# Banded attention and a top-1 mixture of experts on one core: the list of slots spread over the experts' steps, and GpSimd's instructions pinned in the order given

## The chip, the cores and the metric

The kernel runs on one core of one Trainium2 chip. The metric is device time in microseconds (us) of one execution; the number that counts is the median of several runs. An execution has a span (from the first to the last instruction on the core) and a little time around it.

## The reference

Attention over 8 batches, 8 heads, 576 positions and 64 channels. The first four heads see a plain window of 32 positions, the other four a window of 128 positions with a stride of 4. The result, 4608 tokens of 512 channels, goes through a gate that picks one of 8 experts for each token, and through that expert's two layers. Cut to what matters:

```python
scores = where(mask, q @ k.T / sqrt(64), -1e9)
attn = softmax(scores); x = (attn @ v) as 4608 x 512
logits = x @ w_gate + modality_bias[modality_id]
e_idx = argmax(logits); gate_w = softmax(logits)[e_idx]
out[e_idx == e] = gate_w * (relu(x[e_idx == e] @ w1[e]) @ w2[e])
```

## The kernel before, in words

**Attention** is cut into 72 units of 128 rows (nine a batch). A unit's steps lie in different turns of the main loop: `scores` (PE matmuls into `pss`, the mask and the row maximum `nmx` on DVE, and the subtraction `sm` on GpSimd, line 274 by way of the helper `pool`), then `exp` on ACT, `probsT`, `attend`, `normalize`, `store`, and `logits`. Each unit's rows `x_sb` are also written to the scratch tensors `x_dram` by DMAs that GpSimd issues.

**Routing.** When a batch's logits are there, `gating` finds the expert of each token, its place in the expert's list, and scatters token numbers and gate weights into `table` (line 493, six indirect DMAs a batch, issued by GpSimd). Slots of 256 tokens of one expert are the unit of the experts' work. After batch 4 a first list of three slots (0, 1 and 2) is made, so that the experts' work can begin beside the attention's last units. After the last batch `slot_info` makes the list of all other slots and `rest_info` that of the last half slot (`info` and `info_h`, lines 513 to 598: together 37 very small DVE operations on one partition, in pieces that are separated by `yield`). Slots 3 and later cannot be fetched before that list exists.

**A slot's rows** come in a chain: SyncE (SP) reads the slot's place from the list and loads its token numbers (`idt`, line 622); GpSimd gathers the rows with four indirect DMAs into `xr`; SP writes `xr` to the scratch `x_slot` (line 641) and loads it back rearranged as `xg` (four DMAs, line 647); `prepare_x` transposes `xg` on DVE to `xt` (line 786), and ACT and DVE split it into `xh` and `xl` (lines 792 and 793), for each half of 128 tokens in turn. `xr`, `xg` and `xt` have one buffer each.

**The experts' work** is the generator `slots`. A slot has eight groups (f = 0 to 7). A group has 12 matmuls 128x256 of the first layer (line 854), the activation `hh` on ACT and its remainder `hl` on DVE, then the six matmuls 128x512 of the second layer (line 834) of the group two before, then the splits of a piece of `w2` and of the `w1` piece for two groups later (`w2h`, `w1h` on ACT, `w2l`, `w1l` on DVE, lines 802 and 803). A group yields four times, so four steps of the generator make one group. After the second group of a slot, the last slot's two outputs `ys` are scattered to `out` by GpSimd. The helper `ahead`, called twice a group, fetches lists, rows and weights; from the fourth group (f = 3) on it advances `prepare_x` of the next slot, one piece a group. `hold` keeps a slot from being given out before its rows are prepared: it calls `ahead` until they are.

**What sets the order.** PE, DVE, ACT and SP run in the order in which the program gives the instructions (a manual schedule). GpSimd's instructions are placed by a scheduler; the class `InOrder` (line 269) marks them to be kept in program order, and the scatters of `table` are tied to the instruction given last. At the end of the main loop `while not state['routed']` (line 1014) alternates one step of the experts' work with two pieces of the routing of the last batch.

Of the kernel before, what the change touches and what calls it, by code (L numbers as in the profile page):

```python
# [64 lines left out]
def kernel(  # L65
# [53 lines left out]
    def load_qk(b, kd, queue=nc.sync):  # L119
        kn = load_one(b, kd, k)  # L120
        return load_one(b, kd, q, queue), kn
# [17 lines left out]
    state = {('qk', 0, 0): load_qk(0, 0, nc.scalar)}  # L139
# [129 lines left out]
    class InOrder:  # L269


        def __getattr__(self, name):
            def issue(*args, **kw):
                ins = tc.keep_in_program_order(getattr(nc.gpsimd, name)(*args, **kw))  # L274
                state['pool'] = ins.ins
                return ins
            return issue

    pool = InOrder()
# [392 lines left out]
    order = []  # L672
# [250 lines left out]
    def step(share=MOE_RATE / 6):  # L923

        nonlocal credit
        if moe:
            credit += share if state['t'] < NU else 1
            while credit >= 1:
                credit -= 1
                next(moe, None)  # L930

    def advance(some=range(-1, B)):
        for b, task in tasks:
            if b in some:
                next(task, None)
# [76 lines left out]


    while not state['routed']:
        step(1)
        advance()
        advance()
    run(moe)
    man.close()
# [34 lines left out]
```

## Time and profile before

| what | us |
|---|---|
| median of three runs | 710.94 |
| the three runs | 710.84, 721.43, 710.94 |
| the profiled execution | 717.6 |
| its span | 715.9 |
| PE busy in the span | 652.0 (91%) |
| DVE, ACT, GpSimd busy | 496.2, 455.5, 290.7 |

The attention fills about the first 250 us, the experts' work the rest. The two overlap from about 258 us to 287 us; slot 1 of the experts begins at 285 us, slot 2 at 318 us, slot 3 at 341 us. The trace gives, for each instruction, its start, its length, and what ended the idle time of its engine before it.

### The profile page before, as it was taken

The page shows a single profiled execution, that of the slowest core. Times are in us where ns is not written, and L with a number is a line of the kernel's source. Part 1 is how long each engine was busy: PE and PEld are TensorE (multiplying, and loading weights), DVE is VectorE, ACT ScalarE, POOL GpSimd, SP SyncE. Part 2 cuts the span into 40 slices and gives each one's busy share as a digit, 9 for nine tenths or more (in the row PEclk, how much of TensorE's full clock was granted, in tenths as well). Part 3 has the DMA queues.
Part 4 walks back from the last instruction along what each step waited for, and adds up shares of the span by engine and source line. Part 5 has one row for each costly group of instructions (what it writes and reads, how often), then busy time and mean ns, then how long its engine had stood idle before and what let it go on. Part 6 is the DMA issues. An engine that isn't in the chain of part 4 may idle for free. (4 is left out here: it accounts for less than half of the span.)

```text
span 715.9 us, 17885 instructions
## 1 busy us (share of the span) xinstructions
PE 652.0 (91%) x6286; PEld 572.8 (80%) x6286; DVE 496.2 (69%) x1212; ACT 455.5 (64%) x964; POOL 290.7 (41%) x396
## 2 busy tenths in 40 slices
PE   6898899996988789879999999999999999999991
PEld 3687777775876578779999989999999899999880
DVE  1678788785787788687666766677666776667660
ACT  4698799895767665436656555656665565665650
POOL 7344766764658654433333232333213231310110
PEclk7699999999789899989999999999999999999996
DMA  9897698697856964213333863233232336821730
GB/s 163 144 224 176 156 193 177 136 189 131 166 123 159 242 161 79 89 51 98 118 108 100 247 170 115 75 104 119 73 106 75 104 118 169 220 82 46 197 90 12
DMA packets 163233, 94.95 MB, mean 133 GB/s; under 512 B 124144, under 2 KB 143090, under 8 KB 163140
## 3 DMA queue, kind: packets, MB, share of 16 engines
q1 hardware_dynamic: 146612, 63.89, 40.1%
q0 software_dynamic: 11120, 28.64, 13.2%
q10 hardware_dynamic: 5408, 1.24, 1.1%
q8 instruction: 51, 0.84, 0.5%
q14 instruction: 42, 0.34, 0.2%
HBM read 127.52 MB, written 29.39 MB: 219 GB/s over the span
## 5 line engine op out<-in xcount | busy, mean ns | idle before, releaser
L854 PE MATMUL pt<-xh,w1l 128*128 128x256 f32 (+1 forms) x608 | 172.6, 284 | 7.5 <-DVE w1l L803 7.5
L854 PE MATMUL pt<-xl,w1h 128*128 128x256 f32 (+1 forms) x608 | 172.1, 283 | 0.0
L854 PE MATMUL pt<-xh,w1h 128*128 128x256 f32 (+1 forms) x608 | 172.0, 283 | 0.0
L860 ACT ACTIVATE hh<-pt 128x256 fp32r<-128x256 f32 (+1 forms) x152 | 57.6, 379 | 160.3 <-PE pt L854 160.2
L803 DVE TENSOR_TENSOR w2l<-w2q,w2h 128x512 fp32r<-128x512 f32 x152 | 104.8, 689 | 43.1 <-ACT w2h L802 34.7
L274 POOL DMA_INDIRECT xr<-x_dram,idt x74 | 82.8, 1118 | 121.4 <-DMA x_slot<-xr 70.5
L854 PEld LDWEIGHTS pt<-xh,w1l 128*128 128x128 f32 x608 | 116.5, 192 | 8.4 <-DVE w1l L803 8.4
L854 PEld LDWEIGHTS pt<-xh,w1h 128*128 128x128 f32 x608 | 116.4, 191 | 7.2 <-ACT w1h L802 0.6
L854 PEld LDWEIGHTS pt<-xl,w1h 128*128 128x128 f32 x608 | 116.4, 191 | 5.7
L834 PE MATMUL py<-w2h,hh 128*128 128x512 f32 x296 | 118.3, 400 | 0.0
L834 PE MATMUL py<-w2h,hl 128*128 128x512 f32 x296 | 117.2, 396 | 0.0
L834 PE MATMUL py<-w2l,hh 128*128 128x512 f32 x296 | 116.2, 393 | 0.0
L861 DVE SCALAR_TENSOR_TENSOR hl<-pt,hh 128x256 fp32r<-128x256 f32 (+1 forms) x152 | 63.2, 416 | 74.9 <-ACT hh L860 74.9
L274 POOL DMA_INDIRECT out_dram<-ys,idt x37 | 39.8, 1076 | 178.7 <-ACT ys L837 115.8
L803 DVE TENSOR_TENSOR w1l<-w1q,w1h 128x512 fp32r<-128x512 f32 x152 | 103.8, 683 | 3.0 <-ACT w1h L802 3.0
L802 ACT CAST w1h<-w1q 128x512 fp32r<-128x512 f32 x152 | 94.5, 622 | 3.6 <-DMA w1q<-in_moe_w_dram 3.6
L802 ACT CAST w2h<-w2q 128x512 fp32r<-128x512 f32 x152 | 93.1, 612 | 0.0
L274 POOL TENSOR_TENSOR sm<-sm,nmx 128x384 f32<-128x384 f32 x72 | 59.9, 832 | 64.4 <-DVE den L368 49.3
L361 PE MATMUL po<-vw,pT 96*64 96x65 f32 x1152 | 55.9, 239 | 20.3 <-ACT pT L355 16.5
L361 PEld LDWEIGHTS po<-vw,pT 96*64 96x64 f32 x1152 | 44.6, 147 | 32.7 <-ACT pT L355 20.9
L834 PEld LDWEIGHTS py<-w2l,hh 128*128 128x128 f32 x296 | 55.9, 189 | 13.3
L834 PEld LDWEIGHTS py<-w2h,hh 128*128 128x128 f32 x296 | 56.4, 190 | 6.7
(160 smaller groups left out, 1119.9 us busy)
## 6 DMA issues: line engine op xcount, KB each, us to landing
w2q<-in_moe_w_dram SPq DMA_DIRECT2D x76, 512.0 KB
w1q<-in_moe_w_dram SPq DMA_DIRECT2D x152, 256.0 KB
st<-in_k_dram SPq DMA_DIRECT2D x64, 144.0 KB
x_slot<-xr SPq DMA_DIRECT2D x18, 512.0 KB
xg<-x_slot SPq DMA_DIRECT2D x72, 128.0 KB
x_dram<-x_sb POOLq DMA_DIRECT2D x32, 256.0 KB, 3.6
st<-in_q_dram SPq DMA_DIRECT2D x56, 144.0 KB
vw<-in_v_dram SPq DMA_DIRECT2D x8, 576.0 KB
```

The source lines that it names most:

```text
L274: ins = tc.keep_in_program_order(getattr(nc.gpsimd, name)(*args, **kw))
L361: nc.tensor.matmul(out=pov[u * TQ:(u + 1) * TQ, h, :], lhsT=self.pT[:, h, u * TQ:(u + 1) * TQ], rhs=self.vts[kd][:, h, i, :], start=True, ...
L802: nc.scalar.copy(out=hi, in_=raw)
L803: nc.vector.tensor_tensor(out=lo, in0=raw, in1=hi.bitcast(F32), op=ALU.subtract)
L834: nc.tensor.matmul(out=py[u], lhsT=ht[:, us], rhs=wt, start=(f + n == 0), stop=(f + n == FC + 1))
L854: nc.tensor.matmul(out=ph, lhsT=wt[:, c, :], rhs=xt[:, c, 0:cols], start=(c + i == 0), stop=(c + i == KC + 1))
L860: nc.scalar.activation(out=hh, in_=ph, func=AF.Relu)
L861: nc.vector.scalar_tensor_tensor(out=hl, in0=ph, scalar=0.0, in1=hh.bitcast(F32), op0=ALU.max, op1=ALU.subtract)
```

## The change: one piece of routing per three steps, and GpSimd tied

The loop that ends the routing now takes three steps of the experts' work and then one piece of routing, where it took one step and two pieces. Besides, each instruction that goes through the helper `pool` is tied, in the schedule alone and without a semaphore, to the one given before it.

```diff
@@ class InOrder
                 ins = tc.keep_in_program_order(getattr(nc.gpsimd, name)(*args, **kw))
+                if 'pool' in state:
+                    tc.add_manual_dep(ins.ins, state['pool'].name, mybir.DependencyInfo(mybir.DependencyClass.NoSync, mybir.DependencyReason.SCHED_ONLY),
+                                      reason="GpSimd's order")
                 state['pool'] = ins.ins
                 return ins
@@ after the main loop
     while not state['routed']:
-        step(1)
-        advance()
+        for _ in range(3):
+            step(1)
         advance()
     run(moe)
```

Lines after the first hunk are three higher in the changed kernel. The first place that changes is GpSimd's queue near the end of the attention. `sm` is the subtraction that a unit's exponential waits for, `table` a scatter, `xr_5256` the gathers of slot 1's rows. Before:

```order
L493 DMA table_87<-pay_266,dst_4544 41472x3
L274 DMA xr_5256<-x_dram0_84,idt_4215 128x256
L274 DMA xr_5256<-x_dram1_85,idt_4215 128x256
L274 DMA xr_5256<-x_dram0_84,idt_4215 128x256
L274 TENSOR_TENSOR sm_4647<-sm_4647,nmx_4648 128x384
L493 DMA table_87<-pay_266,dst_4544 41472x3
L274 DMA xr_5256<-x_dram1_85,idt_4215 128x256
L274 TENSOR_TENSOR sm_4731<-sm_4731,nmx_4732 128x384
```

Slot 1's four gathers stood here before and between two units' subtractions. In the changed kernel `sm_4647` follows the scatter at once, and the gathers come after the very last subtraction of the attention, `sm_5174`:

```order
L496 DMA table_87<-pay_266,dst_5145 41472x3
L274 TENSOR_TENSOR sm_5174<-sm_5174,nmx_5175 128x384
L274 DMA x_dram0_84<-x_sb_5141 64x256
L274 DMA x_dram1_85<-x_sb_5141 64x256
L274 DMA xr_5256<-x_dram0_84,idt_4215 128x256
L274 DMA xr_5256<-x_dram1_85,idt_4215 128x256
L274 DMA xr_5256<-x_dram0_84,idt_4215 128x256
L274 DMA xr_5256<-x_dram1_85,idt_4215 128x256
L496 DMA table_87<-pay_266,dst_5145 41472x3 x2
```

So the gathers moved behind nine subtractions, and two scatters that stood ahead of `sm_5174` went behind it.

The second place is DVE's queue in slot 1, where the list of slots is made. Before, the rest of the list stood in one block; its end, and the splits that waited behind it:

```order
L598 TENSOR_TENSOR info_5924<-ec 1x25
L590 TENSOR_SCALAR bh<-bh 1x1
L591 SCALAR_TENSOR_TENSOR info_h<-eh,bh 1x1
L593 COPY ec<-last_e 1x1
L594 TENSOR_SCALAR ec<-eh 1x1
L596 COPY last_e<-ec 1x1
L597 CAST info_h<-ec 1x1
L598 TENSOR_TENSOR info_h<-ec 1x1
L803 TENSOR_TENSOR w2l<-w2q_243,w2h 128x512
L803 TENSOR_TENSOR w1l<-w1q_241,w1h 128x512
L786 STREAM_TRANSPOSE xt<-xg 128x4x4x32
```

Now the pieces lie between the groups' own operations, about one a group, from the fourth group of slot 1 to the third of slot 2; a stretch of it:

```order
L545 TENSOR_REDUCE bh<-ch 1x1
L546 TENSOR_TENSOR full<-full,half 1x8
L547 TENSOR_TENSOR full<-full,first 1x8
L548 TENSOR_TENSOR ns<-full,done 1x8
L551 SCALAR_TENSOR_TENSOR cs<-one_277,ns 1x8
L864 SCALAR_TENSOR_TENSOR hl<-pt,hh 128x256
L562 TENSOR_TENSOR ge<-sidx,cs 1x200
L564 TENSOR_REDUCE es<-ge 1x25
L566 TENSOR_TENSOR ns<-full,done 1x8
L806 TENSOR_TENSOR w2l<-w2q_245,w2h 128x512
L806 TENSOR_TENSOR w1l<-w1q_240,w1h 128x512
L864 SCALAR_TENSOR_TENSOR hl<-pt,hh 128x256
```

No operation was added or dropped; the last element of `info` is now written in the second group of slot 2 instead of the fourth group of slot 1.

The third place is DVE's queue at the end of slot 2, where the rows of slot 3 are prepared. Before, each of the four operations stood in a group of its own (f = 3 to 6); the first two of the four groups:

```order
L803 TENSOR_TENSOR w1l<-w1q_241,w1h 128x512
L786 STREAM_TRANSPOSE xt<-xg 128x4x4x32
L861 SCALAR_TENSOR_TENSOR hl<-pt,hh 128x256
L803 TENSOR_TENSOR w2l<-w2q_244,w2h 128x512
L803 TENSOR_TENSOR w1l<-w1q_241,w1h 128x512
L793 TENSOR_TENSOR xl<-xt,xh 128x4x128
```

Now all four stand together behind the last splits of slot 2, since `xg` is not given out before:

```order
L806 TENSOR_TENSOR w2l<-w2q_245,w2h 128x512
L806 TENSOR_TENSOR w1l<-w1q_240,w1h 128x512
L789 STREAM_TRANSPOSE xt<-xg 128x4x4x32
L796 TENSOR_TENSOR xl<-xt,xh 128x4x128
L789 STREAM_TRANSPOSE xt<-xg 128x4x4x32
L796 TENSOR_TENSOR xl<-xt,xh 128x4x128
L864 SCALAR_TENSOR_TENSOR hl<-pt,hh 128x256
```

The `hl` in the last row belongs to the first group of slot 3. On GpSimd the two scatters of slot 1's outputs now stand before the gathers of slot 3 instead of behind them, and on SP `x_slot` of slot 3 stands behind its third `w2` load instead of before its first. From slot 4 on, `xt` and `xl` stand in groups of their own again. PE's order is the same but for the seven small counting matmuls of line 513 (516 now), which come nearly two groups later.

## The prediction

> **What bounds the kernel now.** I read the page first, for the engine that the span hangs on:
>
> ```profile
> PE 652.0 (91%) x6286; PEld 572.8 (80%) x6286; DVE 496.2 (69%) x1212; ACT 455.5 (64%) x964; POOL 290.7 (41%) x396
> ```
>
> PE is the bound, so an edit pays only where PE stands still or runs slowly. Second, the busy time in stretches that I cut at the first-layer matmuls of single groups, around the place where the routing ends, and around GpSimd's gathers for slot 1. Columns: stretch, its length, busy time of PE, its weight loads, DVE, ACT, POOL, granted clock, DMA.
>
> ```profile
> 298.32:302.45 4.13, 3.07 (x19) 2.61 (x18) 3.75 (x19) 1.41 (x4) 3.01 (x3) 1.00 0.05 18
> 302.45:312.78 10.33, 5.10 (x19) 4.37 (x18) 9.62 (x37) 2.25 (x5) 4.37 (x5) 0.67 0.04 3
> 312.78:315.60 2.82, 2.82 (x20) 2.55 (x18) 1.37 (x4) 1.19 (x3) 2.18 (x3) 1.00 0.32 93
> 315.60:318.42 2.82, 2.82 (x20) 2.56 (x18) 2.32 (x5) 1.93 (x5) 1.30 (x1) 1.00 0.31 93
> 228.00:234.30 6.30, 2.96 (x63) 2.47 (x51) 2.29 (x8) 2.59 (x8) 5.18 (x6) 0.98 0.68 112
> 234.30:241.00 6.70, 6.70 (x72) 5.52 (x76) 5.04 (x15) 4.71 (x12) 5.84 (x8) 0.51 1.11 231
> ```
>
> The third and fourth rows are the undisturbed cadence, one group in 2.82 us. The first two rows are also one group each, and take 4.13 and 10.33: together 14.46 for 5.64, a loss of 8.82 us. Third, PE's timeline and the waits in that place:
>
> ```profile
> 299.77 0.39 PE L854 MATMUL pt<-xh,w1l 128*128 128x256 f32 x1 [1.06 <-DVE w1l L803]
> 308.07 0.58 PE L854 MATMUL pt<-xh,w1l 128*128 128x256 f32 x1 [5.23 <-DVE w1l L803]
> 312.78 0.29 PE L854 MATMUL pt<-xh,w1h 128*128 128x256 f32 x1
> ...
> DVE dstf L425 <- POOL t L274: 2.7, 1, 2.7
> ```
>
> Of the 8.8 us, 6.29 are two waits for `w1l`; the rest is mostly the clock, which the second row shows at 0.67. After the long wait, 10 first-layer and 6 second-layer matmuls take 4.71 us (308.07 to 312.78); at the cadence (12 and 6 in 2.82) they take 2.6. So a wait of 5 us costs another 2.1.
>
> Why `w1l` is late stands in DVE's timeline: the routing's small operations are in its way.
>
> ```profile
> 299.64 0.15 DVE L523 TENSOR_SCALAR cn<-po 1x8 int32<-1x8 f32 x1
> ...
> 306.68 0.14 DVE L598 TENSOR_TENSOR info_h<-ec 1x1 int32<-1x1 f32 x1
> 306.74 0.67 DVE L803 TENSOR_TENSOR w2l<-w2q,w2h 128x512 fp32r<-128x512 f32 x1
> 307.35 0.67 DVE L803 TENSOR_TENSOR w1l<-w1q,w1h 128x512 fp32r<-128x512 f32 x1
> ```
>
> **Part 1: the list spread over the steps (gain 8.8).** The 37 small operations take 7.1 us from 299.64 to 306.74, with one `hl` (0.4) among them: 6.7 us. Spread, they come in about ten pieces, one per three steps. A group is four steps, so one piece per 2.1 us and 0.9 us of small work a group. Fits it in? In the two undisturbed groups DVE is busy 1.37 + 2.32 = 3.69 of 5.64 us; with 1.8 more it is 5.5. It fits, narrowly, and `w1l` is made a group and a half ahead of its use, so a piece of delay is covered. `dstf`, which waited 2.7 us for GpSimd, now stands a group later, where its input is old. I take the whole 8.8; the low end, half of it (4.4), is the case where DVE's queue runs over.
>
> **Part 2: slot 3 is late (cost 11.0).** The list's last piece is now written behind `hl` of slot 2's second group. All of slot 3's rows hang on it, and PE's order has slot 3's first matmul right after slot 2. I count from the start H of the activation `hh` of that group (322.87 us in the trace now).
>
> ```profile
> 322.87 0.39 ACT L860 ACTIVATE hh<-pt 128x256 fp32r<-128x256 f32 x1 [1.41 <-PE pt L854]
> ...
> 290.67 0.39 ACT L860 ACTIVATE hh<-pt 128x256 fp32r<-128x256 f32 x1 [2.00 <-PE pt L854]
> 292.33 1.05 POOL L274 DMA_INDIRECT out_dram<-ys,idt  x1 [2.26 <-ACT ys L837]
> 296.32 0.99 POOL L274 DMA_INDIRECT out_dram<-ys,idt  x1 [2.95 <-issue]
> ...
> 308.55 1.56 SPq L622 DMA_DIRECT2D idt<-table  x2
> 311.45 1.06 POOL L274 DMA_INDIRECT xr<-x_dram,idt  x1 [4.77 <-DMA idt<-table]
> 315.44 1.46 POOL L274 DMA_INDIRECT xr<-x_dram,idt  x1 [0.30 <-issue]
> ...
> DMA to landing us min/median/max: 3.1/3.8/8.4
> ...
> 342.85 0.40 SPq L641 DMA_DIRECT2D x_slot<-xr  x1
> 345.64 1.80 SPq L647 DMA_DIRECT2D xg<-x_slot  x4
> ...
> 326.38 1.81 SPq L647 DMA_DIRECT2D xg<-x_slot  x4
> 331.75 0.71 DVE L786 STREAM_TRANSPOSE xt<-xg 128x512 f32<-128x512 f32 x1 [1.02 <-DMA xg<-x_slot]
> ```
>
> The same group in slot 1 shows GpSimd: `hh` at 290.67, first output scatter 1.7 us later, the second 4.0 after the first, 1.0 long. In the new queue both stand before slot 3's gathers, so the first gather is at H + 7.0 with the 0.3 of issue. (By way of the list it would be H + 0.4 for `hh`, 1.4 for `hl` and seven small operations, then SP's reads, and 2.9 from `idt`'s issue to the gather. In the trace now 1.7 lie between the list's end, 306.8, and the first `idt` load, with one `w2` load among them; I take 1.1 for the reads alone, and that is H + 5.8. GpSimd is the later.) The fourth gather starts 4.0 later, lands 3.8 after that (the median of all gathers), H + 14.8. `x_slot` to `xg` 2.8, `xg` to the transpose 5.4: H + 23.0. Then the split, which now has no other work between its steps:
>
> ```profile
> L860 ACT ACTIVATE hh<-pt 128x256 fp32r<-128x256 f32 (+1 forms) x152 | 57.6, 379 | 160.3 <-PE pt L854 160.2
> L861 DVE SCALAR_TENSOR_TENSOR hl<-pt,hh 128x256 fp32r<-128x256 f32 (+1 forms) x152 | 63.2, 416 | 74.9 <-ACT hh L860 74.9
> L786 DVE STREAM_TRANSPOSE xt<-xg 128x512 f32<-128x512 f32 x37 | 26.0, 703 | 1.0 <-DMA xg<-x_slot 1.0
> L793 DVE TENSOR_TENSOR xl<-xt,xh 128x512 fp32r<-128x512 f32 x37 | 25.3, 684 | 1.2 <-ACT xh L792 1.2
> L792 ACT CAST xh<-xt 128x512 fp32r<-128x512 f32 x37 | 23.0, 621 | 7.6 <-DVE info L583 6.0 <-DVE xt L786 1.5
> ```
>
> With one `xt` buffer the two halves are serial: 2 x (0.70 + 0.62 + 0.68) = 4.0, H + 27.0. PE is done with slot 2 at its cadence: `hh` starts 1.6 after its group, so seven groups later is H + 18.1. PE waits 8.9 us, and by the row above such a wait costs 2.1 more: 11.0. On SP, `x_slot` also waits behind a `w2` load that frees with slot 2's sixth group, at about H + 12.7, which is earlier. Low end: if the data are there, the split alone shows. DVE reaches it about 2.2 after slot 2's last `hh` (0.4, then `hl` 0.4, `w2l` and `w1l` 1.4), the split takes 4.0, PE has 1.4 of second-layer work in between: 4.8, with the clock 6.9. High end: a landing of 8.4 instead of 3.8, 15.6. I take the median chain. Slot 4 has a full slot of slack after that, and nothing further is paid.
>
> [...]
>
> **Part 3: GpSimd's order (gain 3.7, of which 2.9 are lost again).**
>
> ```profile
> 228.63 1.09 POOL L274 DMA_INDIRECT xr<-x_dram,idt  x1 [0.30 <-DVE uxl L388]
> 231.35 1.01 POOL L274 DMA_INDIRECT xr<-x_dram,idt  x1 [0.30 <-issue]
> 232.38 0.84 POOL L274 TENSOR_TENSOR sm<-sm,nmx 128x384 f32<-128x384 f32 x1
> ...
> 233.25 0.52 ACT L347 ACTIVATE pe<-sm 128x384 f32<-128x384 f32 x1 [3.71 <-POOL sm L274]
> ...
> 258.15 0.55 DVE L342 TENSOR_REDUCE nmx<-sm 128x4 f32<-128x384 f32 x1
> ...
> 261.65 0.84 POOL L274 TENSOR_TENSOR sm<-sm,nmx 128x384 f32<-128x384 f32 x1
> 262.42 1.16 POOL L274 DMA_DIRECT2D x_dram<-x_sb  x2
> ...
> 274.39 0.70 DVE L786 STREAM_TRANSPOSE xt<-xg 128x512 f32<-128x512 f32 x1
> ```
>
> Three gathers of slot 1 hold back a unit's `sm`; the exponential waits 3.71 us, and PE then runs the next 6.7 us at 0.51. Without them that wait goes: 3.7. The clock could bring 3.3 more (half of 6.7), but slot 0's rows and the weights arrive then by their own DMAs (DMA share 1.11), so I leave it out; ends 2.3 and 7.0. Against that, slot 1's gathers now start behind the last `sm`. That one can start at about 259.0 (`nmx` ends at 258.7, one scatter is left ahead), then 0.8 and the two stores 1.2, 0.3: first gather 261.3, and with the chain of part 2, 4.0 + 3.8 + 2.8 + 5.4: 277.3 for an `xt` that is now taken at 274.39. All of it shifts with the gain, so the lateness stays: 2.9 us, in a stretch where PE has work all the time. I count it in full; with a landing of 3.1 and less for `xg` it is 1. Net gain 0.8.
>
> **The sum**, against the profiled execution's 717.6: -0.8 - 8.8 + 11.0 = +1.4, so 719.0. The median of the runs shown, 710.94, lies 6.7 under that execution; I carry the difference over: **712.3 us**, no change that can be told.
>
> **The rivals.** (a) The rows come early: the gathers land at the fast end and slot 3 pays only the exposed split, 6.9, slot 1's lateness is 1. Then -3.7 + 1.0 - 8.8 + 6.9 = -4.6: 706.3. For it: 3.1 is the smallest landing, and DMA is nearly empty after 300 us (0.04 to 0.32). Against it: `xg` was seen to take 5.4 with little beside it. (b) Slower: slot 3's last gather lands as late as the slowest in the trace, 8.4; PE waits 4.6 us more in one piece, 716.9. The point from which this decides the sign is a cost of part 2 above 9.6 (8.8 + 0.8). For it: nothing covers the chain, every microsecond of it is PE's. Against it: 8.4 is the extreme of 74. (c) DVE runs over: the pieces delay `w1l` by turns and only half of the 8.8 comes back: 716.7. For it: 5.5 of 5.64 us filled; against it, the lead of `w1l`. (d) Nothing happens, since the scheduler had this order before: excluded by the rows of the instruction order, except as a cancellation, which is the forecast.
>
> **How the numbers follow.** Forecast 0.45, (a) 0.25, (b) 0.15, (c) 0.10, 0.05 for what I don't see. The forecast's own range is 708 to 716 (2 us either way in each part). With (a) and (c) the range is 705 to 718. Two per cent, about what a measurement of this kernel can tell from no change, are 14.2 us: below 696.7 the whole gain without any of part 2's cost would not reach (8.8 + 3.7 = 12.5; only with all of part 3's clock, 15.8, would it), and above 725.2 several high ends would have to meet. So faster 0.02, same 0.95, slower 0.03.
>
> **What would show it.** Right: no wait of PE for `w1l` over 1 us near the end of routing; one wait of PE of 6 to 11 us between slots 2 and 3, released by `xl` or `xh`, with a clock near 0.5 behind it; the exponential's wait of 3.71 gone; DVE waiting for `xg` at slot 1's first `xt`. Wrong: PE's wait between the slots under 5 us (then faster, case a), a second such wait at a later slot, or waits for `w1l` still there (case c).

## The result and the profile after

| | before | changed |
|---|---|---|
| median of the runs compared (4 each) | 712.79 | 723.19 |
| lowest and highest | 710.84, 721.43 | 722.34, 724.6 |
| the profiled execution | 717.6 | 724.6 |
| its span | 715.9 | 722.9 |

The ratio is 1.0132 with a 95% interval of 1.0089 to 1.0175, that is 9.4 us (6.3 to 12.5) more than before. Forecast were 1.4 us more against the profiled execution, and 712.3 us with a range up to 718.0. The changed kernel is slower than that, though by less than the 2% that count as slower.

The page of the changed kernel shows the same number of instructions on each engine listed here and, but for GpSimd (8.3 us more), busy times within 2 us; what differs is mainly the idle time. Engines and two groups of section 5 (the last numbers are idle time before the group's instructions, and what ended most of it):

```profile
PE 650.5 (90%) x6286; PEld 570.9 (79%) x6286; DVE 495.1 (68%) x1212; ACT 455.5 (63%) x964; POOL 299.0 (41%) x396
...
L857 PE MATMUL pt<-xh,w1h 128*128 128x256 f32 (+1 forms) x608 | 172.7, 284 | 11.8 <-ACT xh L795 7.8
...
L805 ACT CAST w1h<-w1q 128x512 fp32r<-128x512 f32 x152 | 94.5, 622 | 8.9 <-DMA w1q<-in_moe_w_dram 8.9
```

The first group is the wait before slot 3 that was forecast (7.8 for `xh`) and something besides: 4 us more, for `w1h`. The last group says why: ACT waits 8.9 us for the load of `w1q`. In the kernel before that number was 3.6.

To see **where** the time went I took the starts of ACT's exponentials and of `hh` (one per group of the experts' work) from both timelines and subtracted. They come in the same order in both kernels, so the difference tells what each stretch gained or lost:

| from, to | before: start, start | changed: start, start | changed minus before |
|---|---|---|---|
| start to the 63rd exponential | 0, 226.10 | 0, 224.28 | -1.8 |
| to the 67th exponential | 226.10, 242.70 | 224.28, 239.65 | -1.2 |
| to slot 0, f = 6 | 242.70, 280.83 | 239.65, 280.18 | +2.4 |
| to slot 1, f = 3 | 280.83, 297.13 | 280.18, 296.04 | -0.4 |
| to slot 1, f = 6 (the list) | 297.13, 314.41 | 296.04, 304.95 | **-8.4** |
| to slot 3, f = 2 | 314.41, 348.44 | 304.95, 349.10 | **+10.1** |
| to slot 6, f = 0 | 348.44, 410.29 | 349.10, 410.96 | 0.0 |
| to slot 8, f = 0 | 410.29, 456.15 | 410.96, 459.41 | **+2.6** |
| to slot 15, f = 0 | 456.15, 614.07 | 459.41, 617.33 | 0.0 |
| to slot 16, f = 0 | 614.07, 636.63 | 617.33, 643.62 | **+3.7** |
| to the last `hh` | 636.63, 697.89 | 643.62, 704.88 | 0.0 |

In the stretch before the 63rd exponential GpSimd's order differs in one pair only (slot 0's last gather, at 218.68 us before, now stands behind the subtraction that followed it, so this and not slot 1's gathers is the first place that changes). From that place to the 63rd no exponential waits more than 0.79 us for its subtraction, and the stretch differs by more than that from execution to execution (below). Without it the changed kernel is 8.8 us longer, which is what the times say (9.4). Of the lines above 2.5 us the forecast had all but two: 6.3 us are lost in slots 6 and 15, 100 and 300 us behind the last change in the list's place.

The waits of PE in the changed kernel in these stretches, from its timeline (start, length, and in brackets the wait and what ended it):

```profile
239.45 0.29 PE L410 MATMUL po<-uxl,wgs 128*16 128x128 f32 x1 [4.41 <-DVE uxl L391]
...
275.99 0.23 PE L410 MATMUL po<-uxl,wgs 128*16 128x128 f32 x1 [2.11 <-DVE uxl L391]
...
339.45 0.58 PE L857 MATMUL pt<-xh,w1h 128*128 128x256 f32 x1 [7.77 <-ACT xh L795]
...
423.35 0.39 PE L857 MATMUL pt<-xh,w1h 128*128 128x256 f32 x1 [2.58 <-ACT w1h L805]
...
628.57 0.39 PE L857 MATMUL pt<-xh,w1h 128*128 128x256 f32 x1 [1.43 <-ACT w1h L805]
```

And its stretches (columns as in the prediction): two groups of slot 1 where the list is made, the wait and the stretch behind it before slot 3, and the groups around the lost time in slots 6 and 15.

```profile
303.43:306.25 2.82, 2.82 (x20) 2.56 (x19) 2.72 (x9) 1.41 (x4) 2.28 (x2) 1.00 0.01 0
306.25:309.07 2.82, 2.82 (x20) 2.56 (x19) 2.68 (x10) 1.93 (x5) 2.20 (x2) 1.00 0.10 7
334.80:339.45 4.65, 0.00 (x1) 0.01 (x1) 2.14 (x4) 1.24 (x2) 1.65 (x2) 0.70 0.30 86
339.45:346.90 7.45, 7.31 (x35) 6.46 (x36) 2.77 (x5) 1.90 (x5) 0.00 (x0) 0.73 0.45 143
...
410.96:428.39 17.43, 14.63 (x91) 12.76 (x90) 9.43 (x17) 8.86 (x19) 6.21 (x6) 1.00 0.78 189
617.33:637.98 20.65, 18.99 (x109) 16.54 (x108) 11.86 (x21) 10.27 (x22) 5.90 (x6) 0.92 0.66 152
```

The first two rows show the list made at PE's full cadence with DVE busy 2.7 of 2.82 us. The third is PE standing still, the fourth its clock behind that, 0.73 for 7.45 us. The last two have a DMA share of 0.78 and 0.66: in both places a new expert's weights are loaded.

**How slots 6 and 15 lose.** GpSimd's timeline ahead of slot 6, from the first of its four gathers to the two scatters, before:

```profile
379.12 1.07 POOL L274 DMA_INDIRECT xr<-x_dram,idt  x1 [4.01 <-DMA x_slot<-xr]
...
383.38 1.20 POOL L274 DMA_INDIRECT xr<-x_dram,idt  x1 [0.30 <-issue]
392.21 1.04 POOL L274 DMA_INDIRECT out_dram<-ys,idt  x1 [7.63 <-ACT ys L837]
395.74 1.14 POOL L274 DMA_INDIRECT out_dram<-ys,idt  x1 [2.50 <-ACT w1h L802]
```

and changed, from the second gather to the fourth:

```profile
388.38 1.01 POOL L274 DMA_INDIRECT xr<-x_dram,idt  x1 [0.30 <-issue]
392.88 1.02 POOL L274 DMA_INDIRECT out_dram<-ys,idt  x1 [3.49 <-ACT ys L840]
396.41 1.13 POOL L274 DMA_INDIRECT out_dram<-ys,idt  x1 [2.51 <-ACT w1h L805]
397.85 1.55 POOL L274 DMA_INDIRECT xr<-x_dram,idt  x1 [0.30 <-issue]
399.70 1.02 POOL L274 DMA_INDIRECT xr<-x_dram,idt  x1 [0.31 <-issue]
```

The program gives out one gather a group, so in program order the two scatters of the last slot's outputs stand between a slot's second and third gather. Untied, the scheduler had put all four gathers ahead of the scatters; tied, they stay apart, and the last gather goes out 16 us later (399.70 against 383.38). What SP does with that, before:

```profile
398.40 0.41 SPq L641 DMA_DIRECT2D x_slot<-xr  x1
...
407.36 1.82 SPq L647 DMA_DIRECT2D xg<-x_slot  x4
409.53 2.19 SPq L662 DMA_DIRECT2D w1q<-in_moe_w_dram  x4
```

and changed:

```profile
407.24 0.39 SPq L644 DMA_DIRECT2D x_slot<-xr  x1
...
410.27 1.82 SPq L650 DMA_DIRECT2D xg<-x_slot  x4
412.44 2.19 SPq L665 DMA_DIRECT2D w1q<-in_moe_w_dram  x4
414.98 0.39 SPq L668 DMA_DIRECT2D w2q<-in_moe_w_dram  x1
...
418.10 0.08 SPq L668 DMA_DIRECT2D w2q<-in_moe_w_dram  x1
```

The last two rows are a load that is taken (0.39) and one that is skipped because the next slot has the same expert (0.08). `x_slot` is 8.8 us later, and the load of `w1q`, which stands behind it in SP's queue, is 2.9 later, 2.2 of them later against slot 6's own start (which had moved by 0.7). ACT's split, before and then changed, pays it:

```profile
419.43 0.62 ACT L802 CAST w1h<-w1q 128x512 fp32r<-128x512 f32 x1 [2.42 <-DMA w1q<-in_moe_w_dram]
...
621.98 0.62 ACT L802 CAST w1h<-w1q 128x512 fp32r<-128x512 f32 x1 [1.19 <-DMA w1q<-in_moe_w_dram]
```

```profile
422.68 0.62 ACT L805 CAST w1h<-w1q 128x512 fp32r<-128x512 f32 x1 [5.00 <-DMA w1q<-in_moe_w_dram]
...
627.90 0.62 ACT L805 CAST w1h<-w1q 128x512 fp32r<-128x512 f32 x1 [3.85 <-DMA w1q<-in_moe_w_dram]
```

Each wait is 2.6 to 2.7 us longer. In slot 15 `x_slot` goes out 7.3 us later against the slot's start (612.73 and 617.33, where before has 602.18 and 614.07), the load of `w1q` behind it 1.7 later (617.99 against 613.05), and from that issue to the split it takes 9.9 us instead of 8.9. Before, nearly all of the wait was covered; now PE stands 2.58 us in slot 6 and 1.43 in slot 15. This is read from two traces; whether the tie, the loop or the weights make it is for the experiments.

### The profile page after: what moved, and what is told of

The parts are those of the page before. It is cut to its first block, busy times and chain, and to the rows that moved or that the text cites. A ratio compares the mean times of both kernels' runs of the same rounds, so it can differ in the third digit from the quotient of the medians.

```text
span 722.9 us, 17878 instructions
## 1 busy us (share of the span) xinstructions
PE 650.5 (90%) x6286; PEld 570.9 (79%) x6286; DVE 495.1 (68%) x1212; ACT 455.5 (63%) x964; POOL 299.0 (41%) x396
## 3 DMA queue, kind: packets, MB, share of 16 engines
q0 software_dynamic: 11120, 28.64, 12.5%
## 5 line engine op out<-in xcount | busy, mean ns | idle before, releaser
L274 POOL DMA_INDIRECT xr<-x_dram,idt x74 | 87.6, 1184 | 118.1 <-DMA x_slot<-xr 94.1
L364 PE MATMUL po<-vw,pT 96*64 96x65 f32 x1152 | 53.9, 234 | 18.8 <-ACT pT L358 16.0
L364 PEld LDWEIGHTS po<-vw,pT 96*64 96x64 f32 x1152 | 42.8, 143 | 30.8 <-ACT pT L358 20.8
```

Source lines behind the costliest of these rows:

```text
L364: nc.tensor.matmul(out=pov[u * TQ:(u + 1) * TQ, h, :], lhsT=self.pT[:, h, u * TQ:(u + 1) * TQ], rhs=self.vts[kd][:, h, i, :], start=True, ...
```

## The experiments

Theory A: the terms of the table are separate causes (loop: -8.4 and +10.1; tie: slots 6 and 15, through the split gathers and the weights' loads behind `x_slot`). Against it stand, run by run, that the late phase of the whole does it (B), that a wait is only moved (C), that the tie is slow by itself (D), that late rows do it without weights (E).

All results at one place. "Time" is the ratio of the times less one, by the median of before in the same comparison (712.7 to 718.8 us). The other columns are stretches of the table above, each less the same of before, and their sum from the 63rd exponential to the end (with the stretches not shown, which make 0.5 at most). In the comparison of the four kernels of rows 5 to 8 below the kernel before had its lowest median, 712.67, and three of the four times there are 3 us above what the trace has.

| kernel | time, 95% interval | 63rd exp. to slot 0, f = 6 | list | to slot 3, f = 2 | slots 6, 7 | slot 15 | sum |
|---|---|---|---|---|---|---|---|
| changed | +9.4 (6.3, 12.5) | +1.2 | -8.4 | +10.1 | +2.6 | +3.7 | +8.8 |
| loop alone | +1.0 (-2.4, 4.5) | -0.4 | -8.4 | +10.8 | -0.7 | 0.0 | +0.8 |
| tie alone | +10.5 (5.7, 15.5) | +2.1 | +0.3 | 0.0 | +4.3 | +0.8 | +7.5 |
| changed, four early slots | +1.2 (-1.4, 3.8) | +7.5 | -8.4 | +0.7 | +1.7 | +1.7 | +2.8 |
| changed, gathers in one piece | +4.9 (1.9, 7.9) | +0.1 | -8.4 | +10.4 | -0.7 | +0.2 | +1.1 |
| changed, tie in the attention only | +2.0 (-0.9, 4.9) | -1.9 | -8.4 | +10.3 | -0.7 | 0.0 | -1.1 |
| changed, no reload of weights | +2.7 (0.1, 5.2) | +1.5 | -8.4 | +11.0 | -0.7 | 0.0 | +3.0 |
| before, four early slots | +3.2 (1.1, 5.2) | -1.7 | +2.7 | 0.0 | -0.6 | 0.0 | +0.4 |
| loop with two steps | -1.6 (-4.0, 0.6) | +0.6 | -8.4 | +6.4 | -0.5 | 0.0 | -2.4 |
| loop, four early slots, first timing | -9.9 (-15.4, -4.6) | +0.1 | -8.3 | +0.9 | -0.7 | 0.0 | -8.5 |
| loop, four early slots, timed again | -7.3 (-10.4, -4.3) | -2.0 | -8.3 | +0.9 | -0.7 | 0.0 | -10.5 |
| two steps, four early slots | -3.9 (-6.1, -1.8) | -0.3 | -4.7 | +1.8 | -0.1 | 0.0 | -3.6 |
| both losses taken out | -4.1 (-6.0, -2.2) | -0.4 | -5.5 | +1.5 | +0.2 | 0.0 | -4.6 |

### The loop alone, and the tie alone

The loop of the changed kernel without the first hunk:

```diff
     while not state['routed']:
-        step(1)
-        advance()
+        for _ in range(3):
+            step(1)
         advance()
```

> The loop of three steps and one piece alone, without the tie of GpSimd's instructions. Theory A (the tie makes x_slot late at the two slots where the expert changes, 6.3 us; the loop by itself is -8.4 in slots 1 and 2 and +10 between slots 2 and 3): 1 to 3 us above the kernel before, no loss at slots 6 and 15, one wait of PE of 7 to 8 us between slots 2 and 3. Rival B (the late list shifts everything behind it, and the loss at slots 6 and 15 comes from that phase, not from the tie): about as slow as the changed kernel, 8 to 10 us above before, with the loss of 6 us at slots 6 and 15 there.

Measured: +1.0 us (-2.4 to 4.5). The view of waits (total, times, longest) has one long wait of PE in the experts' work, and none for `w1h`:

```profile
PE pt L854 <- ACT xh L792: 8.0, 1, 8.0
```

Theory A holds and B falls: the list is as late as in the changed kernel, and nothing is lost in slots 6 and 15 (0.7 is even gained).

The first hunk without the loop (the diff is the first one of the change):

> The tie alone, with the loop as it was before. Theory A: 6 to 8 us above the kernel before; the losses of about 3 us each at slots 6 and 15 are there, the two waits for w1l in slot 1 (8.8 us) are still there, no long wait between slots 2 and 3, the exponential's wait of 3.7 us is gone. Rival B: equal to before or up to 1 us faster, and nothing lost at slots 6 and 15.

Measured: +10.5 us (5.7 to 15.5). Its view of waits:

```profile
PE pt L857 <- DVE w1l L806: 9.0, 6, 5.2
ACT w1h L805 <- DMA w1q<-in_moe_w_dram: 7.6, 2, 5.1
...
PE pt L857 <- ACT w1h L805: 2.7, 1, 2.7
```

The waits for `w1l` of the kernel before are all there, no wait for `xh`, and the loss at the weight changes is there without any change of the loop. It is split otherwise (4.3 and 0.8 instead of 2.6 and 3.7), and the sum, 5.1, is a little smaller. The trace's sum, +7.5, lies in the 6 to 8 that were expected, the median of the times above them. The tie, not the loop, makes the slower kernel; nearly everything that the loop does cancels.

### Slot 3's rows taken out of the late list

The changed kernel, and the loop alone, with a first list of four slots:

```diff
-EARLY = ((4, 3),)
+EARLY = ((4, 4),)
```

> The changed kernel with four slots instead of three in the first list, so that slot 3's rows do not hang on the late list. Theory A: the wait of 7 to 8 us of PE between slots 2 and 3 and its clock are gone, 9 to 10 us under the changed kernel, that is about as fast as before (712 to 715); the losses at slots 6 and 15 stay. Rival C (the wait between slots 2 and 3 is only moved: slot 4, now the first of the late list, waits in its place): no gain on the changed kernel, and a wait of PE over 4 us before slot 4.

Measured: +1.2 us (-1.4 to 3.8) above before, 8 under the changed kernel. The wait before slot 3 is gone and did not move to slot 4, so C falls (of the stretch's 10.1 us 0.7 are left, at the change to slot 2, where PE waits 0.44 us for `xl`); the losses at slots 6 and 15 stay, 1.7 each. What was not expected are 7.5 us at the attention's end, where the `xg` of slots 0 and 1 hold DVE longer than in the changed kernel (5.89 and 5.70 us against 4.29 and 3.37):

```profile
242.26 0.71 DVE L789 STREAM_TRANSPOSE xt<-xg 128x512 f32<-128x512 f32 x1 [5.89 <-DMA xg<-x_slot]
...
281.07 0.71 DVE L789 STREAM_TRANSPOSE xt<-xg 128x512 f32<-128x512 f32 x1 [5.70 <-DMA xg<-x_slot]
```

> The loop of three steps and one piece without the tie, and four slots in the first list. Theory A: only the gain of 8.4 in slots 1 and 2 is left, 702 to 706, 7 to 9 us under before. Rival C (the wait moves to slot 4): 0 to 3 us above before. Rival B: loss at slots 6 and 15, so 706 to 712.

Measured: -9.9 us (-15.4 to -4.6) in four runs. That was a small sample, so the same kernel was timed again:

> The same kernel as the run with the loop changed, no tie and four slots in the first list, timed again in five rounds. Theory A: 7 to 11 us under before. If the earlier run was only a good draw of the attention's part: 0 to 4 us under before.

Measured: 709.62 against 716.10, -7.3 us (-10.4 to -4.3). The trace has the whole gain of the list (-8.3) and 0.9 behind it. One row covers the list, slot 2 and the change to slot 3, PE busy 51.54 of 52.00 us at full clock:

```profile
288.00:340.00 52.00, 51.54 (x332) 46.10 (x331) 41.05 (x108) 29.88 (x63) 25.15 (x23) 1.00 0.30 90
```

This version beats both kernels. Its control is the kernel before with the same longer list and nothing else:

> The kernel before with four slots in the first list, nothing else: the control for the run with the loop changed and four early slots. Theory A (the longer first list by itself moves nothing that PE waits for, the gain of that run is the loop's 8.4 us): within 2 us of before, the waits for w1l in slot 1 still there. Rival C (the gain came from the longer list): 5 to 9 us under before.

Measured: +3.2 us (1.1 to 5.2) by the times, +0.4 by the trace (2.7 lost where the list is made, the rest regained). So the longer list is no gain by itself; the two edits pay only together, since the loop alone trades the list's wait for slot 3's.

### The tie's loss undone in three ways

The changed kernel with the four gathers in one piece (the four pauses follow behind them):

```diff
         for u in range(nu):
             for kd in range(2):
                 pool.indirect_dma_start(...)
-                yield
+        for _ in range(2 * nu):
+            yield
```

> The changed kernel with a slot's four gathers given out in one piece, so that the tie no longer puts the two output scatters between the second and the third gather. Theory A (the tie loses 6.3 us at slots 6 and 15 because the last two gathers stand behind the scatters): nothing lost at slots 6 and 15, 5 to 7 us under the changed kernel, 2 to 4 us above before. Rival D (a tied queue is late by itself, whatever stands in it, by its waits in order): the loss at slots 6 and 15 stays within 1 us of the changed kernel's, 8 to 10 us above before.

Measured: +4.9 us (1.9 to 7.9), where A expected 2 to 4; the times alone would not tell that apart from the changed kernel's +9.4, the trace does: slots 6 and 15 lose nothing. GpSimd's timeline ahead of slot 6, from the first gather to the fourth and the first scatter:

```profile
387.74 1.05 POOL L274 DMA_INDIRECT xr<-x_dram,idt  x1 [10.41 <-DMA x_slot<-xr]
...
391.96 1.19 POOL L274 DMA_INDIRECT xr<-x_dram,idt  x1 [0.30 <-issue]
395.13 1.02 POOL L274 DMA_INDIRECT out_dram<-ys,idt  x1 [1.98 <-ACT ys L841]
```

The order of before is back with the tie in place, and `x_slot` goes out 11.9 us ahead of slot 6's first `hh` (401.33 and 413.21) as before (398.40 and 410.29), not 3.7 (407.24 and 410.96). So it is which order is pinned, and not the pinning; D falls.

The changed kernel with the tie ended at the attention's last unit:

```diff
-                if 'pool' in state:
+                if 'pool' in state and state.get('t', 0) < 9 * B:
```

> The changed kernel with the tie only up to the end of the attention's units; the experts' gathers and scatters are left to the scheduler. Theory A: nothing lost at slots 6 and 15, the wait of 7 to 8 us of PE between slots 2 and 3 still there, 5 to 7 us under the changed kernel. Rival B (the loss comes from what the tie does in the attention or from the shifted phase): losses at slots 6 and 15 as in the changed kernel.

Measured: +2.0 us (-0.9 to 4.9), nothing lost at slots 6 and 15, the wait before slot 3 still there (8.0). B falls a second time.

The changed kernel with every slot on the first slot's weights. This leaves out the reload of weights, and with it part of what the kernel must compute:

```diff
-        nc.vector.tensor_tensor(out=info[:, 2, :], in0=ec[:, 1:n + 1], in1=ec[:, 0:n], op=ALU.not_equal)
+        nc.vector.tensor_tensor(out=info[:, 2, :], in0=ec[:, 1:n + 1], in1=ec[:, 1:n + 1], op=ALU.not_equal)
```

> The changed kernel without the reload of weights: the flag that a slot has another expert than the slot before is always zero, so every slot works with the first slot's weights. Theory A (the loss at slots 6 and 15 needs both the late x_slot and the weights' loads that stand behind it on SP): nothing lost at slots 6 and 15, all waits of ACT for w1q gone, 6 us or more under the changed kernel; the wait of PE between slots 2 and 3 still there, 6 to 9 us. Rival E (the loss comes from the late rows themselves, xg and xt): the loss of about 3 us at each of slots 6 and 15 stays.

Measured: +2.7 us (0.1 to 5.2). Its gathers are still split by the scatters, and `x_slot` still goes out late (403.51, 7.6 us ahead of slot 6's first `hh`, where before has 11.9 and the changed kernel 3.7), but the same two stretches run at PE's cadence:

```profile
411.11:425.21 14.10, 14.10 (x91) 12.78 (x90) 9.64 (x17) 8.85 (x19) 4.62 (x4) 1.00 0.17 59
614.15:631.07 16.92, 16.92 (x109) 15.34 (x108) 11.97 (x21) 10.26 (x22) 4.73 (x4) 1.00 0.22 77
```

This run alone would not settle E, since without the loads its rows are only about half as late. The changed kernel's own trace does. From slot 8 to slot 14 it loses nothing, although in slot 9, for one, `x_slot` goes out 14.2 us after the slot's first `hh` (496.13 and 481.97) instead of 10.4 (489.07 and 478.71). And in its whole run DVE waits for `xg` three times, before slots 0, 1 and 3, never in slots 6 and 15:

```profile
DVE xt L789 <- DMA xg<-x_slot: 11.0, 3, 4.3
```

So E falls: the late rows alone cost nothing there, they cost through the weights that stand behind them on SP. Both are needed, the late `x_slot` and the loads behind it.

### How early the list must be

The loop with two steps per piece, untied:

```diff
-        for _ in range(3):
+        for _ in range(2):
             step(1)
```

> Two steps of the experts' work per piece of routing instead of three, without the tie. In the order of instructions the list is then written three groups (8.5 us) earlier than with three steps, and the four operations that prepare slot 3's rows stand in groups of their own. Theory A (the wait between slots 2 and 3 is only the lateness of the list): that wait of 8 us is gone or under 1.5, the gain of 8.4 in slots 1 and 2 stays or loses up to 2 to waits for w1l, 6 to 9 us under before. Rival F (the pieces need three steps each to hide: DVE runs over at two): waits for w1l of 3 to 5 us in slot 1 again, 2 to 5 us under before.

Measured: -1.6 us (-4.0 to 0.6), less than either expected, though the interval reaches F's 2 to 5 us. The list's gain is whole (-8.4), but 6.4 of the 10 are still paid behind it, in two places. At the change to slot 2, 1.9: there the pieces of the list fill DVE (busy 4.45 of 4.69 us with 22 operations, 303.48 to 308.17) and PE waits 1.62 us for `xl`, which is F's cause at a smaller price and at another tile. The other 4.5 come before slot 3, and DVE's timeline tells why:

```profile
321.06 0.68 DVE L803 TENSOR_TENSOR w1l<-w1q,w1h 128x512 fp32r<-128x512 f32 x1
326.39 0.71 DVE L786 STREAM_TRANSPOSE xt<-xg 128x512 f32<-128x512 f32 x1 [4.65 <-DMA xg<-x_slot]
...
327.93 0.68 DVE L803 TENSOR_TENSOR w1l<-w1q,w1h 128x512 fp32r<-128x512 f32 x1
```

The list is three groups earlier and so is `xg`, but the program now places slot 3's first transpose three groups earlier too (behind the splits of f = 4 of slot 2, in the three-step kernel behind those of f = 7). There DVE waits 4.65 us for rows that PE would need only at the slot's end, and `w1l` stands behind it in DVE's queue (327.93). PE then waits 1.92 us for `w1l`, and its clock is 0.67 in the 4 us behind:

```profile
326.60:330.00 3.40, 1.49 (x10) 1.34 (x9) 3.40 (x7) 1.93 (x4) 0.00 (x0) 0.89 0.13 39
330.00:334.00 4.00, 3.55 (x14) 2.73 (x13) 3.55 (x7) 1.93 (x4) 0.00 (x0) 0.67 0.00 0
```

> Two steps per piece, no tie, and four slots in the first list. Theory A (with the list early enough by either means the other adds nothing): within 2 us of the kernel with two steps alone and of the one with three steps and four early slots, 6 to 10 us under before. Rival G (the longer first list costs 2 to 3 us where the loop ends, as the control with four early slots showed in slot 1): 4 to 7 us under before.

Measured: -3.9 us (-6.1 to -1.8), just outside G's range and far from A's. With the longer list only 4.7 of the list's 8.4 come back and 1.8 are paid behind it, these again at the change to slot 2 (PE waits 1.51 us for `xl`). What is missing of the 8.4 is an order on GpSimd once more: slot 3's four gathers (293.68 to 297.69) and two scatters stand ahead of the routing's `t` (304.82), `dstf` on DVE waits 4.14 us for it, and PE waits 1.88 us for the `w1l` behind. With three steps the same gathers stand there and `t` comes as late (4.7 us after the `hh` of f = 3 in both), but `dstf` stands later on DVE: it waits only 2.14 us, and PE not at all for `w1l` there. Three steps with four early slots stays the better pair.

### Both losses out of the changed kernel

The loop and the tie, with gathers in one piece and four early slots (the two diffs above together):

> The changed kernel, loop and tie, with both of its losses taken out: a slot's four gathers given out in one piece, and four slots in the first list. Theory A (the parts add: -8.4 in slots 1 and 2, no wait between slots 2 and 3, nothing lost at slots 6 and 15; the tie is left with its effect at the attention's end alone, 0 to +7 us in the runs so far): 2 to 8 us under before. Rival D (the tie costs something of its own behind the attention): losses at slots 6 and 15 again, equal to before or above it.

Measured: -4.1 us (-6.0 to -2.2). Nothing is lost at slot 15 and 0.2 at 6 and 7, so D falls there a second time. But the list gives 5.5 here instead of 8.4, and the trace says why: given out in one piece and tied, slot 3's four gathers (305.01 to 309.28) stand on GpSimd between the second output scatter (303.72) and the routing's `t` (310.68), which in the changed kernel follows that scatter by 2.0 us (296.48 and 298.44). `dstf` waits 4.94 us for `t`, and PE 2.64 us for the `w1l` behind it (313.51); the 1.5 of the next column are the group behind that (4.35 us instead of 2.82). So by this one trace the order that is pinned still costs 4.4 us where the list is made.

## Why the prediction was wrong, point by point

- **Bound.** PE; right. Where rows show a loss (the list, slot 3, slots 6 and 15), PE stood or ran slowly.
- **Part 1, -8.8: right.** -8.4 in the changed kernel and in five others with three steps (5.5 where everything is put together). Rival (c), DVE running over, did not come: two groups in a row at 2.82 us with DVE at 2.7.
- **Part 2, +11.0: right in kind, 0.9 too much.** +10.1. PE's wait is 7.77 where 8.9 were forecast, and the clock behind it 0.73 for 7.45 us. Counted from H (313.41 in the changed kernel), `x_slot` went out at 14.8 (forecast 14.8), `xg` at 17.6 (17.6), the first transpose started at 22.5 (23.0), and PE at 26.0 instead of 27.0, its wait ending with `xh` and not with the second `xl`. With the rows early 0.7 to 0.9 is left, so the cause is shown: 9.4 (changed kernel) to 9.9 (loop alone) hang on the late list.
- **Part 3, -0.8: wrong in sign, small.** The exponential's wait of 3.71 us is gone; the time saved (5.3 between the 63rd exponential and the 66th) was given back almost at once, because slot 0's rows, which that wait had covered, are now late in their turn. DVE stands before slot 0's first transpose, and PE behind it (4.41 us, quoted above):

```profile
238.38 0.71 DVE L789 STREAM_TRANSPOSE xt<-xg 128x512 f32<-128x512 f32 x1 [4.29 <-DMA xg<-x_slot]
...
274.92 0.71 DVE L789 STREAM_TRANSPOSE xt<-xg 128x512 f32<-128x512 f32 x1 [3.37 <-DMA xg<-x_slot]
```

  The second row is slot 1's lateness, forecast at 2.9. From the 63rd exponential to slot 1, f = 3, the changed kernel lost 0.7 instead of gaining 0.8. In the other kernels tied as a whole it lies between -0.8 and +7.1, in the untied ones between -2.4 and +0.2; what sets the 7.1 is open beyond the row quoted there.
- **The step that failed: "Slot 4 has a full slot of slack after that, and nothing further is paid."** 6.3 us are paid, in slots 6 and 15, for which the sum has no term. The part on the change had it in view: "On GpSimd the two scatters of slot 1's outputs now stand before the gathers of slot 3 instead of behind them". I took that as a fact about slot 3, where the late list hides it, and costed the tie in the attention alone. But the tie holds for every later slot, and I did not carry the changed order forward to the slots where the slack is not there: in the rows of before, ACT already waited 2.42 and 1.19 us for `w1q` in exactly these two slots. The rival's "DMA is nearly empty after 300 us (0.04 to 0.32)" was read from rows that end at 318 us; in slots 6 and 15 the changed kernel's share is 0.78 and 0.66. A queue that is already late at the place where something is moved in front of it should have been the first suspect.
- **The sum.** -8.4 + 10.1 + 0.7 = +2.5 (the terms are rounded), near the +1.4 of the forecast, partly because the misses of parts 2 and 3 (-0.9 and +1.5) pull against each other; the 6.3 make it +8.8. The time given besides, 712.3, rested on a median of three runs (710.94); later medians of the same kernel were 712.7 to 718.8.
- **Rivals.** (a) and (c) did not come. (b) put a slower outcome on the late landing of a gather; the gather does land late for PE, but later in the program and by way of SP's queue. What I wrote would show me wrong, "a second such wait at a later slot", is what came.

## What to carry to other kernels

Pinning an order is an edit at every place where that order differs from the one the scheduler chose, not only at the place for which it is made: compare the queues to the end of the program, and look first at the stages where a load is already waited for. A transfer held back on one queue can be paid by what stands behind its consumer on the next one: here, at slot 6, the last gather went out 16.3 us later behind two scatters, the store `x_slot` on SP 8.8 us later, and the load of `w1q` behind it, which had nothing to do with any of them, 2.9 us later. Moving a producer earlier (the list in two steps) can let the program place its consumer just as much earlier, and then the engine waits for it with other work behind it (here DVE 4.65 us for `xg`, and PE 1.92 us for the `w1l` behind).

## What the runs showed of the hardware that was not expected

The clock behind a wait is not set by the wait's length alone. Slot 6 of the changed kernel and of the tie alone have nearly the same wait of PE for `w1h` (2.58 and 2.71 us); behind the first the next two groups run at full clock, behind the second at 0.91 and 0.65. The changed kernel, then the tie alone:

```profile
423.20:425.57 2.37, 2.00 (x13) 1.79 (x14) 2.24 (x5) 1.41 (x5) 0.89 (x1) 1.00 0.06 13
425.57:428.39 2.82, 2.82 (x19) 2.56 (x18) 2.81 (x5) 1.94 (x5) 2.21 (x3) 1.00 0.40 137
```

```profile
427.02:429.50 2.48, 2.12 (x13) 1.91 (x14) 2.36 (x5) 1.40 (x4) 0.96 (x1) 0.91 0.05 14
429.50:433.74 4.24, 4.24 (x19) 3.65 (x19) 2.74 (x5) 1.93 (x4) 2.50 (x3) 0.65 0.34 117
```

And in slot 15 of the changed kernel a wait of only 1.43 us is followed by a group at 0.68 (4.07 us long instead of 2.82):

```profile
631.09:635.16 4.07, 4.07 (x19) 3.48 (x19) 2.63 (x5) 1.93 (x5) 2.55 (x2) 0.68 0.15 61
```

So the shortest of the three waits (1.43) has a slower clock behind it than the one of 2.58. A group loses 1.3 to 1.4 us by it. In slot 15 of the changed kernel this weighs more than the wait: PE is busy 18.99 us with the 109 matmuls that take 16.92 in the run without reload, 2.1 us more, beside 1.7 us of standing. It is part of why slots 6 and 15 share their loss differently from kernel to kernel. In the kernel before, the two waits of PE for `w1l` in slot 1 (1.06 and 5.23 us) have these clocks behind them, 1.00 and 0.52:

```profile
299.77:302.45 2.68, 2.68 (x16) 2.42 (x17) 2.30 (x15) 1.19 (x3) 2.07 (x3) 1.00 0.01 1
308.07:312.78 4.71, 4.71 (x16) 4.18 (x17) 4.45 (x11) 2.03 (x4) 1.06 (x1) 0.52 0.04 3
```

What sets the clock behind a wait, no run here shows.

The stretch up to the 63rd exponential took 220.55 us in the profiled execution of the loop with two steps, and 229.83 in that of two steps with four early slots, though the two kernels differ only in how many slots the first list has, and 5.7 of the 9.3 us stand already at the 40th exponential, before that list. In the two profiled executions of the loop with four early slots, one and the same kernel (713.9 and 701.86 us), it took 230.86 and 220.89: 10.0 of the 12.0 us between them. Where that comes from is not shown, nor whether all of the scatter between runs (before: 707.26 to 724.1 over all comparisons) lies there. It is why a few microseconds are told here by stretches of the trace and by ratios with their intervals, and not by two medians.
